# One stretch of 64x64 matmuls per unit in an attention-then-mixer kernel

## The chip, the cores and the metric

The kernel runs on one core of one Trainium2 chip. The metric is the time of one execution on the device in microseconds (us). The core has a matrix engine (PE, TensorE, whose weight loads are profiled apart as PEld), a vector engine (DVE), a scalar engine (ACT), POOL (GpSimd), which here starts the loads, and SP (SyncE), which here starts transposing DMAs and stores. PE writes into PSUM, which DVE and ACT read.

## The reference

Eight batches of 448 tokens, 12 heads of 64 and thus 768 columns:

```
attn = sigmoid(q k^T / 8 - log 448)            # q, k, v: (8, 12, 448, 64), no softmax
x    = attn v, heads side by side              # (8, 448, 768)
h    = relu(x^T w_tok1) w_tok2                 # tokens: 448 -> 256 -> 448
u    = x + h^T
out  = u + relu(u w_ch1) w_ch2                 # channels: 768 -> 1536 -> 768
```

## The kernel before

Tokens lie as 7 blocks (j) of 64. A batch is done in three units (u = 0, 1, 2) of four heads each: head pair hi (0, 1) of two groups g (0, 1). So there are 24 units, numbered c = 3b + u. Operands are fp16, sums fp32.

The first stage of a unit: **qk** (L153) multiplies, for each j, a 64-token block of k with all of q: four matmuls with 64 rows and 64 columns of weights, each in its own quarter of the array (called a quad below), and 448 columns streamed. Each fills one of two PSUM tiles "qk"; ACT reads it through the sigmoid (L168) into att. **av** (L178) sums att times v over the 7 blocks, a quad for each; DVE casts the two sums into xT (L197) and copies the last 64 tokens once more behind them (L201). **xtrans_dma** (L211) transposes xT by a DMA on SP into xn. **tok1** (L233) multiplies by w_tok1: from unit 4 on its 64-token remainder is one quad (L254, with_scores) and the rest full 128x128 matmuls (L265); ACT applies ReLU (L279). **ytrans** (L281) multiplies by w_tok2 with full matmuls (L286), and DVE adds x (L293), which gives u, two of six 128-column slices per unit.

The second stage of a batch, once all of u is there: **ch1** (L311), 12 products cb of six full matmuls with 448 columns (L318), DVE ReLU to h2 (L326); **ch2** (L333), six products (t, half) of 12 full matmuls with 384 columns (L341), DVE adds u (L351) from un, the transposed u that **utrans** (L298) makes by a DMA on SP; and **ch2_last** (L374), the last 64 tokens, in pairs of 128x64 matmuls (L386, adds L411). Stores go out on SP.

The order is written out by hand (manual schedule): each engine works in the order of the code. The loop of L609 does for each c: scores 0 and 1, av of unit c-1, score 2, a share of second-stage pieces (work(1)), scores 3 and 4, the remainder quad and tok1 of unit c-2, work(2), scores 5 and 6, work(3), ytrans of unit c-2. So each unit enters the 64x64 arrangement three times. `stage2` deals the second stage of a batch in pieces of three matmuls, about a third of its weight for each unit (`shares`), from u=2 of the next batch on.

Behind a piece, a step of `through_dma` may be dealt: DVE copies k and q of the next batch into another order (relayout, L106, three for each), and then a DMA on SP transposes them (L119). When q's is there, POOL copies two of its elements (gate, L680), and behind that starts the loads of v for the next batch and k and q for the one after it.

PSUM has eight banks: four for the two qk tiles, four under the tag "m" with bufs=4 that everything else takes in turn.

Of the kernel before, what the change touches and what calls it, by code (L numbers as in the profile page):

```python
# [26 lines left out]
def kernel(  # L27
# [45 lines left out]

    raw, rel, tr = {}, {}, {}
# [60 lines left out]
    def pe_transpose(b, t, u, j0=0, j1=NJ, on_scalar=False):  # L135
        if j0 == 0:
            tps[t] = pp.tile([128, NJ, 128], FP16, tag="m", bufs=4, name=f"tp_{t}_{b}_{u}")
        ps = tps[t]
        for j in range(j0, j1):
            for hi in range(2):  # L140
                nc.tensor.transpose(  # L141
                    out=ps[64 * hi : 64 * hi + 64, j, :],
                    in_=raw[b, t][:, u, hi, j, :],
                    identity=ident[:, :],
                )
        dst, src = tr_tile(b, t)[:, u, j0:j1, :], ps[:, j0:j1, :]
        if on_scalar:
            nc.scalar.activation(out=dst, in_=src, func=COPYF)
        else:
            nc.vector.tensor_copy(out=dst, in_=src)  # L150
# [27 lines left out]
    def av(b, u, j0=0, j1=NJ):  # L178
        if j0 == 0:
            xa[b, u] = [  # L180
                pp.tile([128, 512], FP32, tag="m", bufs=4, name=f"xa_{b}_{u}_{g}")
                for g in range(2)
            ]
        ps = xa[b, u]
        for j in range(j0, j1):
            for g in range(2):
                for hi in range(2):
                    nc.tensor.matmul(  # L188
                        out=ps[g][64 * hi : 64 * hi + 64, 0:S],
                        lhsT=raw[b, "v"][64 * g : 64 * g + 64, u, hi, j, :],  # L190
                        rhs=att[b, u][64 * g : 64 * g + 64, hi, j, :],
                        start=(j == 0),
                        stop=(j == NJ - 1),
                    )
        if j1 == NJ:
            for g in range(2):
                nc.vector.tensor_copy(  # L197
                    out=xTs[b % 2][:, u, g, 0:S], in_=ps[g][:, 0:S]
                )
            if NU * b + u >= N_FIRST:  # L200
                nc.vector.tensor_copy(  # L201
                    out=xTs[b % 2][:, u, :, S:512], in_=xTs[b % 2][:, u, :, S - 64 : S]
                )
# [13 lines left out]
    def xtrans(b, u):  # L217
        ps = pp.tile([128, 4, 2, 128], FP16, tag="m", bufs=4, name=f"xb_{b}_{u}")
        for g in range(2):
            for t in range(4):  # L220
                nc.tensor.transpose(  # L221
                    out=ps[:, t, g, :],
                    in_=xTs[b % 2][:, u, g, 128 * t : 128 * t + 128],
                    identity=ident[:, :],
                )
        nc.vector.tensor_copy(
            out=xn_tile(b)[:, u, :, :, :].rearrange("s g t d -> s t g d"),
            in_=ps[:, :, :, :],
        )
# [3 lines left out]
    def tok1(b, u, relu_on_vector=False, tcbs=range(2), with_scores=False):  # L233

        if tcbs[0] == 0:
            if u == 0:
                h1[b] = pa.tile(
                    [128, 2, 2, NU, 128], FP16, tag="h1", bufs=2, name=f"h1_{b}"
                )
            if with_scores:  # L240
                tks[b] = [
                    pp.tile([128, 2, 2, 128], FP32, tag="m", bufs=4, name=f"tk_{b}_{u}_{tcb}")[
                        :, 0, :, :
                    ]
                    for tcb in range(2)
                ]
            else:
                one = pp.tile([128, 2, 2, 128], FP32, tag="m", bufs=4, name=f"tk_{b}_{u}")
                tks[b] = [one[:, tcb, :, :] for tcb in range(2)]
        ps = tks[b]  # L250
        for tcb in tcbs if with_scores else []:
            part = slice(64 * tcb, 64 * tcb + 64)
            for g in range(2):
                nc.tensor.matmul(  # L254
                    out=ps[tcb][64 * g : 64 * g + 64],
                    lhsT=w1[part, 3, 128 * tcb + 64 * g : 128 * tcb + 64 * g + 64],
                    rhs=xn[b][part, u, :, 3, :],
                    start=True,
                    stop=False,
                )  # L260
        for tcb in tcbs:
# [10 lines left out]
        for tcb in tcbs:  # L272
            dst, src = h1[b][:, tcb, :, u, :], ps[tcb]
            if relu_on_vector:
                nc.vector.tensor_scalar(
                    out=dst, in0=src, scalar1=0.0, scalar2=None, op0=MAX
                )
            else:
                nc.scalar.activation(out=dst, in_=src, func=RELU)  # L279

    def ytrans(b, u):  # L281
        for g in range(2):
            db = NU * g + u
            ps = pp.tile([128, 512], FP32, tag="m", bufs=4, name=f"yt_{b}_{db}")
# [26 lines left out]
    def ch1(b, cb, d0=0, d1=NDB):  # L311
        if cb == 0 and d0 == 0:
            h2[b] = pa.tile([128, NCB, S], FP16, tag="h2", bufs=1, name=f"h2_{b}")
        if d0 == 0:
            acc[b, cb] = pp.tile([128, 512], FP32, tag="m", bufs=4, name=f"c1_{b}_{cb}")
# [9 lines left out]
        if d1 == NDB:  # L325
            nc.vector.tensor_scalar(  # L326
                out=h2[b][:, cb, :], in0=ps[:, 0:S], scalar1=0.0, scalar2=None, op0=MAX
            )

# [3 lines left out]
    def ch2(b, t, half, n0=0, n1=NCB):  # L333
        cols = slice(DH * half, DH * half + DH)
        if n0 == 0:
            if half == 0:
                outs[b, t] = pa.tile([128, D], FP32, tag="outs", bufs=4, name=f"o_{b}_{t}")
            acc[b] = pp.tile([128, 512], FP32, tag="m", bufs=4, name=f"c2_{b}_{t}_{half}")
# [9 lines left out]
        if n1 < NCB:  # L348
            return
        if b in un:  # L350
# [6 lines left out]
        else:  # L357
            for n in range(NU):
                nc.tensor.matmul(  # L359
                    out=ps[:, 128 * n : 128 * n + 128],  # L360
                    lhsT=uts[b % 2][:, NU * half + n, 128 * t : 128 * t + 128],
                    rhs=ident[:, :],
                    start=False,
                    stop=(n == NU - 1),
                )
# [7 lines left out]

    def ch2_last(b, n0=0, n1=NCB):  # L374
        final = b == B - 1
        if n0 == 0:
            acc[b] = [
                pp.tile([128, 512], FP32, tag="m", bufs=4, name=f"c2_{b}_3_{g}")
# [107 lines left out]
    def stage2(b):  # L486
        for cb in range(NCB):
            for d in range(0, NDB, 3):
                yield 3 * S, lambda cb=cb, d=d: ch1(b, cb, d, d + 3)
        groups = [(t, half) for t in range(3) for half in range(2)]  # L490
        if b == 0:
            groups.sort(key=lambda g: g[1])
        for t, half in groups:
            for n in range(0, NCB, 3):
                yield 3 * DH, lambda t=t, half=half, n=n: ch2(b, t, half, n, n + 3)
        for n in range(0, NCB, 3):
            yield 3 * DH, lambda n=n: ch2_last(b, n, n + 3)

# [12 lines left out]
    def new_heat():  # L511
        heat[0] = pp.tile([128, 512], FP32, tag="m", bufs=4, name="heat")
# [91 lines left out]

    ON_DMA = range(N_FIRST, N_CYCLES)
    ON_PE = 2 * NU + 1
    starts = [N_FIRST] + [NU * b + 5 for b in range(1, B - 1)] + [N_CYCLES + 1]
    pending, copies = [], []
    for c in range(N_FIRST, N_CYCLES + 1):  # L609
        b, u = divmod(c, NU)  # L610
        here = c < N_CYCLES
        before = divmod(c - 1, NU)
        mixed = [n for n in (c - 2, c - 1) if (n == c - 1) != (n in ON_DMA) or not here]
        if c in starts:
            lot = starts.index(c)
            first = c
            pending = list(stage2(lot))[4 if c == N_FIRST else 0 :]
            total = sum(w for w, f in pending)


            shares = {0: [9, 9, 6, 6], 1: [12, 9, 9]}.get(lot, [10, 10, 10])
            spent = [0, 0]

        def work(share):
            goal = 3 * sum(shares[: c - first]) + share * shares[c - first]
            while pending and spent[0] < total * goal / 90:
                w, f = pending.pop(0)
                f()
                spent[0] += w
                spent[1] += 1  # L630
                if copies and (c < 3 * NU or spent[1] % 2 == 0):
                    copies.pop(0)()

        if here:
            qk(b, u, 0)
            qk(b, u, 1)
# [3 lines left out]
        if here:  # L640
            qk(b, u, 2)
        if c == 2 * NU + 2:
            copies += through_dma(3, 0)[NU + 1 :]
        work(1)
# [5 lines left out]
        if here:  # L650
            qk(b, u, 3)
            qk(b, u, 4)
        early = [n for n in mixed if here and n < c - 1]
        for n in early:
            tok1(*divmod(n, NU), with_scores=True)
# [4 lines left out]
        work(2)  # L660
        if u == 2 and b > 1:
# [4 lines left out]
        if here:  # L666
            qk(b, u, 5)
            qk(b, u, 6)
        if b > 2 and u == 0 and b + 1 < B:
            copies = through_dma(b + 1, 0)  # L670
        work(3)
        if c == N_FIRST:
            nc.gpsimd.dma_start(out=w1[64:128, 3, :], in_=tok_rows[NJ - 1])
        for n in mixed:
# [4 lines left out]
        if here and u == 2 and b + 1 < B:  # L679
            nc.gpsimd.tensor_copy(  # L680
                out=gate[:, :], in_=tr[b + 1, "q"][:, NU - 1, NJ - 1, 126:128]
            )
            if b > 1:
                load(b + 1, "v", v, 0, NU)
            for t, src in (("k", k), ("q", q)):
                if b + 2 < B:
                    load(b + 2, t, src, 0, NU)
    assert not copies
    utrans(B - 1)
    for w, f in pending:  # L690
# [33 lines left out]
```

## Time and profile before

| | before |
|---|---|
| three runs, us | 368.52, 368.86, 370.37 (median 368.86) |
| profiled execution: time / span, us | 368.45 / 366.7 |
| PE busy, matmuls | 359.0 us (98%), 3308 |
| PEld (weight loads) busy | 194.5 us (53%), 3308 |
| DVE busy, instructions | 186.0 us (51%), 343 |
| ACT busy, instructions | 172.5 us (47%), 214 |
| granted PE clock in the 40 slices | 9 tenths or more throughout |
| L318 (ch1) / L341 (ch2) / L161 (qk) / L188 (av) busy, us | 115.3 / 100.3 / 53.1 / 37.4 |
| read from and written to device memory | 43.45 MB / 11.01 MB |

The span runs from the first to the last instruction of the profiled execution. A row of a timeline gives start, duration, engine, line, what is written and read, and the count of like instructions merged; in brackets the idle time of the engine before it and what ended that. A row of waits gives who waited for whom, the total in us, the number of times and the longest. A row of the chain gives start, duration and what the end of the kernel depended on then. PE's instructions overlap: the end of each is modelled, so the distance of starts tells the pace.

### The profile page before, as it was taken

The numbers are of one execution on the slowest core, as the hardware profiler recorded it, in microseconds if no ns is written. First come the engines' busy times: TensorE is split into PE (matmuls) and PEld (weight loads), VectorE is DVE, ScalarE is ACT, GpSimd is POOL, SyncE is SP. The second block draws the span as 40 slices with busy tenths as digits, with TensorE's granted clock in tenths as the row PEclk, the third lists the DMA queues.
The fourth block names the chain that finished last, engine by engine and source line by source line (L and its number), as shares of the span: only waits on it lengthen the run. The fifth ranks groups of instructions, "written<-read, shape, count | busy, mean of one in ns | idle before, by whom it ended". The sixth has DMA issues, their size and how long they took to land.

```text
span 366.7 us, 7619 instructions
## 1 busy us (share of the span) xinstructions
PE 359.0 (98%) x3308; PEld 194.5 (53%) x3308; DVE 186.0 (51%) x343; ACT 172.5 (47%) x214; POOL 52.6 (14%) x91
## 2 busy tenths in 40 slices
PE   8899999999999999999999999999999999999995
PEld 5555555555555554555455554555445555555563
DVE  3366647258455456465455455473463355444531
ACT  2995565665455455455455445445545544000000
POOL 8865500110310040002100040000100000000000
PEclk9999999999999999999999999999999999999999
DMA  8999999999995999779991999749931344136014
GB/s 145 170 190 206 203 204 188 133 195 212 192 188 110 197 170 193 98 146 194 181 183 45 176 186 192 104 96 203 196 60 33 84 93 88 30 84 154 0 43 109
DMA packets 103953, 52.01 MB, mean 142 GB/s; under 512 B 76016, under 2 KB 100848, under 8 KB 103920
## 3 DMA queue, kind: packets, MB, share of 16 engines
q1 hardware_dynamic: 78880, 29.70, 43.3%
q0 software_dynamic: 24816, 21.50, 38.1%
q8 instruction: 26, 0.43, 0.5%
q10 hardware_dynamic: 224, 0.33, 0.3%
q14 instruction: 7, 0.06, 0.1%
HBM read 43.45 MB, written 11.01 MB: 149 GB/s over the span
## 4 chain that ended last, share of the span: by engine, by line
PE 94%; ACT 4%; DVE 1%; issue 0%
PE c L318 30%; PE c L341 26%; PE qk L161 10%; PE xa L188 8%; PE tk L265 5%; PE yt L286 5%; PE c L386 5%; ACT att L168 3%; PE heat L503 1%; PE tp_k L141 1%; PE tk L254 1%; PE tp_q L141 1%; PE xb L221 0%; DVE xT L197 0%; PE c L359 0%
## 5 line engine op out<-in xcount | busy, mean ns | idle before, releaser
L168 ACT ACTIVATE att<-qk,att_bias 128x896 f16<-128x896 f32 x168 | 158.4, 1008 | 130.8 <-PE qk L161 130.8
L318 PE MATMUL c<-ut,c 128*128 128x448 f16 x576 | 115.3, 353 | 0.0
L341 PE MATMUL c<-c,h 128*128 128x384 f16 x576 | 100.3, 326 | 0.0
L326 DVE TENSOR_SCALAR h<-c 128x448 f16<-128x448 f32 x96 | 59.7, 624 | 59.6 <-PE c L318 58.7
L318 PEld LDWEIGHTS <-c 128*128 128x128 f16 x576 | 54.2, 98 | 55.2 <-issue 9.1
L341 PEld LDWEIGHTS <-h 128*128 128x128 f16 x576 | 54.5, 98 | 40.6 <-issue 6.8
L161 PE MATMUL qk<-tr_q,tr_k 64*64 64x448 f16 x672 | 53.1, 361 | 2.1 <-ACT att L168 2.0
L351 DVE TENSOR_TENSOR o<-un,c 128x384 f32<-128x384 f16 x42 | 23.3, 554 | 58.7 <-PE c L341 58.6
L188 PE MATMUL xa<-att,raw_v 64*64 64x448 f16 x672 | 37.4, 350 | 0.0
L197 DVE CAST xT<-xa 128x448 f16<-128x448 f32 x48 | 27.7, 619 | 17.7 <-PE xa L188 17.7
L161 PEld LDWEIGHTS <-tr_k 64*64 64x64 f16 x672 | 15.8, 104 | 28.3 <-issue 25.6
L293 DVE TENSOR_TENSOR ut<-xT,yt 128x448 f16<-128x448 f16 x48 | 27.4, 614 | 5.9 <-PE yt L286 5.7
L188 PEld LDWEIGHTS <-raw_v 64*64 64x64 f16 x672 | 22.5, 107 | 9.9 <-issue 1.1
L680 POOL COPY gate<-tr_q 128x2 f16<-128x2 f16 x6 | 1.1, 183 | 182.9 <-DMA tr_q<-rel_q 163.0
L286 PE MATMUL yt<-w,h 128*128 128x448 f16 x96 | 22.1, 353 | 0.0
L265 PE MATMUL tk<-xn,w 128*128 128x256 f16 (+1 forms) x156 | 21.7, 274 | 0.0
L279 ACT ACTIVATE h<-tk 128x256 f16<-128x256 f32 x42 | 13.8, 387 | 13.4 <-PE tk L265 13.4
L407 ACT ACTIVATE o<-c 64x384 f32<-64x384 f32 x1 | 0.5, 485 | 40.6 <-PE c L397 40.6
L265 PEld LDWEIGHTS <-w 128*128 128x128 f16 (+1 forms) x156 | 13.3, 97 | 8.3 <-issue 6.2
L386 PE MATMUL c<-c,h 128*64 128x384 f16 x192 | 17.3, 328 | 0.0
L95 POOL DMA_DIRECT2D raw_q<-in_q_dram x26 | 16.7, 658 | 2.3 <-POOLq L708 0.8
L95 POOL DMA_DIRECT2D raw_k<-in_k_dram x24 | 15.3, 657 | 7.4 <-DMA c<-in_moe_w_ch_dram 4.3
(49 smaller groups left out, 136.0 us busy)
## 6 DMA issues: line engine op xcount, KB each, us to landing
out_dram<-o SPq DMA_DIRECT2D x48, 192.0 KB, 2.8
c<-in_moe_w_ch_dram POOLq DMA_DIRECT2D x4, 1152.0 KB, 15.3
raw_v<-in_v_dram POOLq DMA_DIRECT2D x12, 336.0 KB, 6.8
raw_k<-in_k_dram POOLq DMA_DIRECT2D x10, 336.0 KB, 9.3
raw_q<-in_q_dram POOLq DMA_DIRECT2D x10, 336.0 KB, 12.3
raw_q<-in_q_dram POOLq DMA_DIRECT2D x14, 112.0 KB, 6.2
out_dram<-o SPq DMA_DIRECT2D x15, 96.0 KB, 2.9
raw_k<-in_k_dram POOLq DMA_DIRECT2D x12, 112.0 KB, 6.1
```

The lines of the kernel that those rows point to most:

```text
L95: nc.gpsimd.dma_start(out=dst.rearrange("p u hi j e -> p (u hi) (j e)"), in_=heads.rearrange("h (p j) e -> p h (j e)", j=NJ),)
L161: nc.tensor.matmul(out=ps[64 * g : 64 * g + 64, hi, 0:S], lhsT=tr[b, "k"][64 * hi : 64 * hi + 64, u, j, 64 * g : 64 * g + 64], rhs=tr[b, " ...
L168: nc.scalar.activation(out=att[b, u][:, :, j, :], in_=ps[:, :, 0:S], func=SIGMOID, bias=bias_t[:, :], scale=att_scale,)
L188: nc.tensor.matmul(out=ps[g][64 * hi : 64 * hi + 64, 0:S], lhsT=raw[b, "v"][64 * g : 64 * g + 64, u, hi, j, :], rhs=att[b, u][64 * g : 64 ...
L197: nc.vector.tensor_copy(out=xTs[b % 2][:, u, g, 0:S], in_=ps[g][:, 0:S])
L265: nc.tensor.matmul(out=ps[tcb], lhsT=w1[rows, t, cols], rhs=xn[b][rows, u, :, t, :], start=(t == 0 and not with_scores), stop=(t == (2 if ...
L286: nc.tensor.matmul(out=ps[:, 0:S], lhsT=h1[b][:, tcb, g, u, :], rhs=w2[:, tcb, :, :], start=(tcb == 0), stop=(tcb == 1),)
L293: nc.vector.tensor_tensor(out=uts[b % 2][:, db, 0:S], in0=xTs[b % 2][:, u, g, 0:S], in1=ps[:, 0:S], op=ADD)
L318: nc.tensor.matmul(out=ps[:, 0:S], lhsT=c1[:, BY_UNIT[d], 128 * cb : 128 * cb + 128], rhs=uts[b % 2][:, BY_UNIT[d], 0:S], start=(d == 0), ...
L326: nc.vector.tensor_scalar(out=h2[b][:, cb, :], in0=ps[:, 0:S], scalar1=0.0, scalar2=None, op0=MAX)
L341: nc.tensor.matmul(out=ps[:, 0:DH], lhsT=h2[b][:, cb, 128 * t : 128 * t + 128], rhs=c2[:, cb, cols], start=(cb == 0), stop=(cb == NCB - 1 ...
L386: nc.tensor.matmul(out=ps[g], lhsT=h2[b][:, n, 384:448], rhs=c2[:, n, DH * g : DH * g + DH], start=(n == 0), stop=(n == NCB - 1 and not ad ...
```

## The change

From unit 9 (batch 3) on, the loop is another one. Each unit has one stretch in the 64x64 arrangement: all seven scores, av of the unit before, the remainder quad of the token product, and a pair of second-stage products that are cut into quads. `quads` issues four 64x64 matmuls: in turn 0 row half r of the weights goes to product r, in turn 1 to product 1 - r; the first turn runs over all slices before the second. A pair in ch1 is done wholly so (six slices, two turns); a pair in ch2 has eight of its twelve slices in quads and four as full matmuls after the stretch (`rest`).

The second stage is dealt anew: all of ch1 in u=2, ch2 for t=0 and ch2_last in the next u=0, ch2 for t=1 and 2 in u=1. The steps of copies and transposes for k and q stand behind every second piece of u=0, 1 and 2. utrans is issued early in u=2, ahead of that unit's xtrans_dma. Unit 8 does all of ch1 of batch 1, with three visits as before.

The four "m" banks get names m0 to m3 with one buffer each, and `bank` hands them out in turn, skipping a bank with an open sum; from unit 9 on at_bank is set by hand, so that pairs and second-stage products begin at m2 and av, the token product and ytrans at m0 and m1.

```diff
+    at_bank, open_bank = [0], [None]
+    def bank(shape, dtype, name):
+        if at_bank[0] == open_bank[0]:
+            at_bank[0] = (at_bank[0] + 1) % 4
+        tag = f"m{at_bank[0]}"
+        at_bank[0] = (at_bank[0] + 1) % 4
+        return pp.tile(shape, dtype, tag=tag, bufs=1, name=name)
...
-                pp.tile([128, 512], FP32, tag="m", bufs=4, name=f"xa_{b}_{u}_{g}")
+                bank([128, 512], FP32, f"xa_{b}_{u}_{g}")
...
+    def quads(ps, n, turn, lhsT, rhs, first, last):
+        for r in range(2):
+            p = r ^ turn
+            part = slice(64 * r, 64 * r + 64)
+            for m in (0, 64):
+                nc.tensor.matmul(
+                    out=ps[p][m : m + 64, 0:n],
+                    lhsT=lhsT(p, part, m),
+                    rhs=rhs(p, part),
+                    start=(first and turn == 0),
+                    stop=(last and turn == 1),
+                )
+    def ch1_pair(b, cb):
+        if cb == 0:
+            h2[b] = pa.tile([128, NCB, S], FP16, tag="h2", bufs=1, name=f"h2_{b}")
+        ps = [bank([128, 512], FP32, f"c1_{b}_{cb + p}") for p in range(2)]
+        def step(turn, d):
+            quads(
+                ps,
+                S,
+                turn,
+                lambda p, part, m: c1[
+                    part, BY_UNIT[d], 128 * (cb + p) + m : 128 * (cb + p) + m + 64
+                ],
+                lambda p, part: uts[b % 2][part, BY_UNIT[d], 0:S],
+                d == 0,
+                d == NDB - 1,
+            )
+            if turn == 1 and d == NDB - 1:
+                for p in range(2):
+                    ch1_out(b, cb + p, ps[p])
+        turns = [[lambda t=t, d=d: step(t, d) for d in range(NDB)] for t in range(2)]
+        return turns[0], turns[1], lambda: None
...
+    def ch2_pair(b, t):
+        outs[b, t] = pa.tile([128, D], FP32, tag="outs", bufs=4, name=f"o_{b}_{t}")
+        ps = [bank([128, 512], FP32, f"c2_{b}_{t}_{p}") for p in range(2)]
+        n_quads = 8
+        def step(turn, n):
+            quads(
+                ps,
+                DH,
+                turn,
+                lambda p, part, m: h2[b][part, n, 128 * t + m : 128 * t + m + 64],
+                lambda p, part: c2[part, n, DH * p : DH * p + DH],
+                n == 0,
+                False,
+            )
+        def rest():
+            for p in range(2):
+                for n in range(n_quads, NCB):
+                    nc.tensor.matmul(
+                        out=ps[p][:, 0:DH],
+                        lhsT=h2[b][:, n, 128 * t : 128 * t + 128],
+                        rhs=c2[:, n, DH * p : DH * p + DH],
+                        start=False,
+                        stop=(n == NCB - 1),
+                    )
+                ch2_out(b, t, p, ps[p])
...
+    ONE_RUN = 3 * NU
...
-    for c in range(N_FIRST, N_CYCLES + 1):
+    for c in range(N_FIRST, ONE_RUN):
...
-            shares = {0: [9, 9, 6, 6], 1: [12, 9, 9]}.get(lot, [10, 10, 10])
...
+            if c == N_FIRST:
+                pending, shares = stage2(0, by_half=True)[4:], [9, 9, 6, 6]
+            else:
+                pending, shares = list(pieces_ch1(1)), [30]
...
+        if c + 1 == ONE_RUN:
+            at_bank[0] = 0
         for n in mixed:
             ytrans(*divmod(n, NU))
...
+    for c in range(ONE_RUN, N_CYCLES):
+        b, u = divmod(c, NU)
+        before, ahead = divmod(c - 1, NU), divmod(c - 2, NU)
+        lot = b - 1 if u == 2 else b - 2
+        at_bank[0] = 2
+        if u == 2:
+            turn0, turn1, rest = ch1_pair(lot, 0)
+            work = pieces_ch1(lot, 2)
+        elif u == 0:
+            turn0, turn1, rest = ch2_pair(lot, 0)
+            work = pieces_last(lot)
+        else:
+            turn0, turn1, rest = ch2_pair(lot, 1)
+            work = pieces_ch2(lot, [(2, 0), (2, 1)])
+        part = len(turn1) * 2 // 3
+        qk(b, u, 0)
+        qk(b, u, 1)
+        for f in turn0:
+            f()
+        qk(b, u, 2)
+        if u == 2:
+            utrans(b - 1)
+        av(*before, 0, 4)
+        qk(b, u, 3)
+        av(*before, 4, NJ)
+        xtrans_dma(*before)
+        qk(b, u, 4)
+        for f in turn1[:part]:
+            f()
+        qk(b, u, 5)
+        for f in turn1[part:]:
+            f()
+        at_bank[0] = 0
+        tok_tail(*ahead)
+        qk(b, u, 6)
+        rest()
+        tok1(*ahead, with_scores=True)
+        at_bank[0] = 2
+        if u == 0 and b + 1 < B:
+            copies = through_dma(b + 1, 0)
+        for n, (w, f) in enumerate(work):
+            f()
+            if copies and n % 2 == 1:
+                copies.pop(0)()
+        at_bank[0] = 0
+        ytrans(*ahead)
+        if u == 2 and b + 1 < B:
+            gated_loads(b)
...
+    c, lot = N_CYCLES, B - 2
+    groups = [(t, half) for t in range(3) for half in range(2)]
+    work = [f for w, f in [*pieces_ch2(lot, groups), *pieces_last(lot)]]
+    before, ahead = divmod(c - 1, NU), divmod(c - 2, NU)
+    av(*before)
+    xtrans_dma(*before)
+    for f in work[:12]:
+        f()
+    tok1(*ahead)
+    for f in work[12:16]:
+        f()
+    tok1(*before)
+    for f in work[16:20]:
+        f()
+    ytrans(*ahead)
+    ytrans(*before)
     utrans(B - 1)
```

`tok_tail` is the remainder quad taken out of tok1, `ch1_out` and `ch2_out` are the DVE outputs taken out of ch1 and ch2, and `pieces_ch1`, `pieces_ch2` and `pieces_last` are the parts of `stage2`. `gated_loads` is the gate with its loads, put into a function.

## The prediction

> **What bounds the kernel now.** I read the page's busy shares and its chain first, then the chain in order of time, the timeline of one steady stretch, and last the waits and the landings of the loads.
>
> ```profile
> PE 359.0 (98%) x3308; PEld 194.5 (53%) x3308; DVE 186.0 (51%) x343; ACT 172.5 (47%) x214; POOL 52.6 (14%) x91
> ...
> PE 94%; ACT 4%; DVE 1%; issue 0%
> ```
>
> PE carries the span; ACT and DVE are half idle. From the waits, and from the chain in order of time:
>
> ```profile
> PE qk L161 <- ACT att L168: 2.0, 5, 0.5
> ```
>
> ```profile
> 25.91 0.51 PE tp_k L141 x14
> ...
> 334.93 13.72 PE c L318 x72
> 348.66 11.70 PE c L341 x72
> ```
>
> PE waits for ACT only in the first 21 us; later it never waits. A full-array matmul of 448 columns takes 13.72/72 = 0.19 us (single starts lie 0.189 apart), one of 384 columns 11.70/72 = 0.1625. So time can go only where PE spends more than these pitches. The timeline of a steady stretch (start, duration, engine, line, count):
>
> ```profile
> 211.44 0.93 PE L286 MATMUL yt<-w,h 128*128 128x448 f16 x4
> 211.55 1.14 DVE L411 TENSOR_TENSOR o<-un,c 64x384 f32<-64x384 f16 x2 [1.52 <-PE c L386]
> ...
> 225.44 0.92 PE L286 MATMUL yt<-w,h 128*128 128x448 f16 x4
> ...
> 226.29 0.57 PE L161 MATMUL qk<-tr_q,tr_k 64*64 64x448 f16 x8
> ...
> 226.70 1.49 PE L188 MATMUL xa<-att,raw_v 64*64 64x448 f16 x28
> 226.79 2.80 ACT L168 ACTIVATE att<-qk,att_bias 128x896 f16<-128x896 f32 x3 [2.36 <-PE qk L161]
> ...
> 228.31 3.58 PE L318 MATMUL c<-ut,c 128*128 128x448 f16 x18
> ...
> 231.82 0.57 PE L161 MATMUL qk<-tr_q,tr_k 64*64 64x448 f16 x8
> ...
> 232.44 0.83 PE L265 MATMUL tk<-xn,w 128*128 128x256 f16 x6
> ```
>
> From 225.44 to 228.31 there are 4 full matmuls and 10 quads (four 64x64 matmuls side by side: 3 score quads, 7 of L188), 14 x 0.189 = 2.65 us, but 2.87 passed. By single starts, entering the 64x64 mode costs 0.093 (282 ns for 189), the first quad 0.025 (214), leaving 0.103 and the first full matmul 0.011: **0.232 us per visit**. From 228.31 to 231.82, 18 full matmuls take 3.51 for 3.40: the same 0.093 at the next entry. A unit (one c) has three visits.
>
> **The change, part by part.** The profiled execution took 368.45 us (span 366.7, 1.75 around it); the median of the runs shown, 368.86, is 0.4 above it.
>
> *Visits.* Units 9 to 23, fifteen, go from three visits to one: 30 x 0.232 = **-6.96 us**. The visits to 128x64 for L386 stay.
>
> *Quads for full matmuls.* A pair in ch1 is 12 quads of 448 columns in place of 12 full matmuls, five times; L188 shows such quads 189 ns apart with fresh weights each: 0. A ch2 pair is 16 quads of 384 columns for 16 full ones (8 stay full in rest), ten times. No quad of 384 columns is in the trace. From below, 384 columns take 162.5 (L341, and pairs of L386 in 128x64 mode); from above, L188's 189, with as many instructions for a quad. 160 x 0.0265 = 0 to +4.24 us. I take 0: eight instructions in 162.5 ns are 20 ns each, and the transposes (L141, 56 ns for two loads and two matmuls) issue one per 14 ns. PE gets 660 more matmuls and loads; the densest 5.2 us now holds 220 instructions, a run will hold some 250.
>
> The Trainium skill ("TensorE: Matmul & The Clock Gate", Part 3) says that a weight load overlaps a running matmul only if it is for another row group. By that, all 220 new quads would pay for their loads. This trace disagrees: L188 reloads the same tile every 189 ns.
>
> *Scores paced by ACT.* ACT starts 0.50 after the first score quad (226.29 to 226.79) and runs at 0.897 per tile (2.80 for three with its tail); a score quad needs the tile two before it read, 1.06 after that read began (8.65 to 9.71 early on). So scores 2 to 6 cannot start before 1.56, 2.45, 3.35, 4.25, 5.14 in the run. PE would be there, in a ch2 run, at 1.70, 2.65, 3.41, 4.41, 5.20: no wait. In a ch1 run at 1.54, 2.50, 3.26, 4.30, 4.97: waits of 0.02, 0.09, 0.17, in all 0.28. Only batch 7 pays it (**+0.28**); in the others a later start, next, covers it.
>
> *Joint from u=1 to u=2.* The copies of k and q (L106, 0.53 each in a row) are dealt behind every second piece, so one stands on DVE between the add of the unit's last product (L351) and the two adds of L293. Counted from the next unit's first score: L351 ends at -0.10 (it starts 0.36 after its last matmul, and lasts 0.55), the copy at 0.47, the L293 adds at 1.04 and 1.61. The sixth slice (d=5) of the ch1 pair reads the second add's result; PE is there at 0.403 + 5 x 0.189 = 1.35 and waits to 1.68: 0.33. All PE work behind it waits; the casts and ACT have slack. Batches 3 to 6 have copies: 4 x 0.33 = **+1.32**.
>
> *Joint from u=0 to u=1.* Now L386 to L286 to L161 with two L411 adds ending 0.39 after the first score (212.69 against 212.30). The new copy goes behind them (0.96), the adds of L293 end at 1.53 and 2.10. The run's av takes banks 0 and 1 that these adds read, at 1.89; it waits to 2.16. The pair's bank 2 waits 0.04 for L411, so 0.27 in all: 4 x 0.27 + 0.04 = **+1.12**. From u=2 to u=0 no copy is left: adds end at 1.04, no wait.
>
> *Banks.* In a run tail and tok1 want banks 0 and 1 after both casts: last av quad + 0.40 + 1.17 + 0.05, 1.62 later; PE arrives 1.70 later in a ch1 run, 1.87 in a ch2 run. At the end of unit 8 the counter is set to 0, and counting allocations from the start the last ch1 sum sits in bank 1, read until 1.02 after its last matmul starts, while the second ytrans wants it at 0.57: **+0.5** once. Elsewhere round robin as before: bounds 0 to +0.2 for a unit, from the shown L326 (0.62).
>
> *Queues.* On SP the transpose of u (L300) moves ahead of that of x (L212) in u=2, and the k and q copies and transposes move from u=0 and 1 to u=0, 1 and 2, two, four and two of eight steps. SP is held up to 13 us by L300 while loads run (217.32), else 3.7. L300 now starts when no load runs, x's transpose is behind it by at most 4 us and is read a unit later. tr_q is issued about 8.7 into u=2 and lands 5.8 later (207.67 to 213.43): 14.5 of 18.4, so the next scores don't wait. The gate on POOL and the six loads behind it move from the start of u=2 to 14.6 into it:
>
> ```profile
> 213.55 0.18 POOL L680 COPY gate<-tr_q 128x2 f16<-128x2 f16 x1 [37.78 <-DMA tr_q<-rel_q]
> ...
> 215.29 1.35 POOL L95 DMA_DIRECT2D raw_k<-in_k_dram  x2
> ...
> 217.32 13.22 SPq L300 DMA_TRANSPOSE un<-ut  x1
> ```
>
> The second half of k landed 226.05, 12.5 after the gate: 27.1, which is 8.7 into the next u=0, where DVE's copy of k waits for it at 7.4 and must be done by 9.74 (L411). Cost 0, margin 0.4 us.
>
> *Tail.* Unit 24 and the last batch have the same pieces in another order: 0.
>
> Sum: -6.96 + 0.28 + 1.32 + 1.12 + 0.5 = -3.74; 368.45 - 3.74 = 364.7. As the median was 0.4 above the profiled execution, I say **365.0 us**.
>
> **Rivals.**
> 1. *Joints free.* If DVE clears sooner or the waits overlap, all 6.96 stays: 361.5 to 363. For it: each wait is 0.3 us, less than one DVE copy, so a copy that is dealt one piece earlier would clear it. Against: in every stretch read, DVE does its work in the order of the code. 0.10.
> 2. *Quads of 384 columns run at 189.* +4.24: 369. For it: twice the weight loads of L386; against: the 14 ns of the transposes. 0.10.
> 3. *More joints wait* (ACT behind ReLU, casts late by the 0.08 margin of the ch1 run, named banks), 0.2 more in each of 15 units: +3.0, 367 to 370. 0.14.
> 4. *Slower: k lands late.* DVE in u=0 is stuck on the copy of k; L411, the adds, and then av of the next run move by as much, in units 12, 15, 18. Each us beyond the 0.4 costs 3 us; it beats the gain when k is 1.25 + 0.4 = 1.65 us later than reckoned, and shows as slower from 2.3 us: 371 and more. For it: the gates of 130.27 saw k at 143.78, 13.5 later, 1 us worse. Against: L300, which shared those loads' time, is gone from there. 0.08.
> 5. *Weight loads are not hidden* in the new quads: 220 x 0.107 (the load row of 64x64) = +23.5: 388. L188 speaks against. 0.03; this is the case that the skill's sentence above describes.
>
> **How the numbers follow.** Forecast 0.55, its own range 363 to 367. A measurement tells 0.5% (1.84 us) from no change: faster is below 367.0. Forecast, rival 1 and 0.03 of rival 3 make 0.68 faster; rival 2 and 0.09 of rival 3 make 0.19 same; rivals 4 and 5 and 0.02 of rival 3 make 0.13 slower. The range 362.4 to 369.8 leaves out rivals 4 and 5 and half of 1.
>
> **What would show it.** One entry to 64x64 per unit from unit 9; PE busy share unchanged. The quads of ch2_pair 162 ns apart. Gaps of 0.33 before the last slices of the ch1 pair's first turn, released by DVE's L293 line, and of 0.27 before av in u=1; none in u=0. k's landing before 9 us into u=0. Wrong, if quads of 384 lie over 180 apart, if DVE waits for raw_k, or if ACT releases scores by more than 0.3 in a ch2 run.

## The result, and the profile after

The changed kernel takes 366.68 us (median of 13 runs, 366.38 to 368.61) against 368.76 for the kernel before (13 runs): a ratio of 0.9949, with a 95% interval of 0.9931 to 0.9967. That is 2.1 us, where 3.7 were forecast. The profiled executions, 366.46 and 368.45, differ by 1.99, and it is this difference that is taken apart below. Some executions of most kernels here take 1.5 to 2 us longer than the rest, at a mean granted clock of 0.993 to 0.995 in place of 0.997 to 1.0; the medians are over all, and one such execution, that of the fixed turn alone, is the one profiled below (its granted clock is 0.50 to 0.65 between 20 and 24 us).

The page of the changed kernel, busy shares and the head of the chain:

```profile
span 364.7 us, 8938 instructions
...
PE 354.8 (97%) x3968; PEld 207.2 (57%) x3968; DVE 186.2 (51%) x343; ACT 171.3 (47%) x214; POOL 52.8 (14%) x91
...
PE 89%; DMA 4%; POOL 4%; ACT 1%; DVE 0%; issue 0%; POOLq 0%
```

PE still carries the span, with 660 matmuls more. Its share of the chain fell from 94% to 89%, and loads came in with 8%. Before one believes that the loads are the matter now, the waits of PE must be read (who waited for what: us in total, times, longest):

```profile
PE qk L174 <- ACT att L181: 2.0, 5, 0.5
...
PE c L333 <- DVE h L345: 0.7, 1, 0.7
...
PE tp_q L154 <- DMA raw_q<-in_q_dram: 0.7, 1, 0.7
...
PE tp_q L154 <- DVE xT L210: 0.5, 1, 0.5
...
PE yt L300 <- DVE h L345: 0.3, 1, 0.3
```

Only the first row was there before, with the same 2.0. The other four are new, and three of the four lie before 50 us, in a part of the kernel where the order of the work was not changed. (Waits of a single quarter of the array don't appear here as idle time of PE; they show only in the length of a stretch.)

The stretch of a unit u=0 in the timeline (start, duration, engine, line, count of like instructions), PE alone:

```profile
148.15 0.57 PE L174 MATMUL qk<-tr_q,tr_k 64*64 64x448 f16 x8
148.55 1.47 PE L357 MATMUL c<-c,h 64*64 64x384 f16 x32
149.85 0.36 PE L174 MATMUL qk<-tr_q,tr_k 64*64 64x448 f16 x4
150.04 0.93 PE L201 MATMUL xa<-att,raw_v 64*64 64x448 f16 x16
...
153.23 0.28 PE L260 MATMUL tk<-xn,w 64*64 64x256 f16 x4
153.34 0.36 PE L174 MATMUL qk<-tr_q,tr_k 64*64 64x448 f16 x4
153.63 1.15 PE L462 MATMUL c<-c,h 128*128 128x384 f16 x6
```

One entry, one way out, 5.48 us from 148.15 to 153.63. The eight quads of 384 columns start at 148.55 and the next score at 149.85: 1.30/8 = 0.1625 each, the pace of full matmuls of that size. 14 quads of 448 columns at 0.189, 16 at 0.1625, one of 256 at 0.109 and 0.128 for the first quad and the way out make 5.48: this stretch waits for nothing. From unit 9 on one batch takes 41.4 us (230.26 to 271.66 between the ytrans of u=2), where it took 42.2 (225.61 to 310.07 for two).

Matched matmul by matmul against the kernel before, PE is 0.66 us late at the q transpose of 24.73, 1.37 late at that of 31.82 (some of which it makes good), 2.18 late at a ch1 matmul at 48.38, and then steadily so up to unit 8. (0.09 of this is there ahead of the first of these waits.)

### The profile page after: what moved, and what is told of

Same layout as the page of the kernel before. It is cut to its first block, busy times and chain, and to the rows that moved or that the text cites. A ratio compares the mean times of both kernels' runs of the same rounds, so it can differ in the third digit from the quotient of the medians.

```text
span 364.7 us, 8938 instructions
## 1 busy us (share of the span) xinstructions
PE 354.8 (97%) x3968; PEld 207.2 (57%) x3968; DVE 186.2 (51%) x343; ACT 171.3 (47%) x214; POOL 52.8 (14%) x91
## 4 chain that ended last, share of the span: by engine, by line
PE 89%; DMA 4%; POOL 4%; ACT 1%; DVE 0%; issue 0%; POOLq 0%
PE c L333 27%; PE c L402 15%; PE c L357 11%; PE qk L174 9%; PE xa L201 8%; PE yt L300 5%; PE tk L279 5%; PE c L486 5%; PE c L462 4%; DMA raw_q<-in_q_dram 2%; DMA raw_v<-in_v_dram 2%; POOL raw_q L108 1%; POOL raw_k L108 1%; POOL raw_v L108 1%; ACT att L181 1%
## 5 line engine op out<-in xcount | busy, mean ns | idle before, releaser
L181 ACT ACTIVATE att<-qk,att_bias 128x896 f16<-128x896 f32 x168 | 155.6, 1015 | 119.7 <-PE qk L174 119.0
L333 PE MATMUL c<-ut,c 128*128 128x448 f16 x516 | 100.6, 353 | 0.7 <-DVE h L345 0.7
L333 PEld LDWEIGHTS <-c 128*128 128x128 f16 x516 | 49.6, 98 | 48.4 <-issue 4.4
L174 PE MATMUL qk<-tr_q,tr_k 64*64 64x448 f16 x672 | 60.3, 357 | 2.1 <-ACT att L181 2.0
L402 PE MATMUL c<-c,h 128*128 128x384 f16 x336 | 58.1, 326 | 0.0
L402 PEld LDWEIGHTS <-h 128*128 128x128 f16 x336 | 32.1, 98 | 21.7 <-issue 1.8
L201 PE MATMUL xa<-att,raw_v 64*64 64x448 f16 x672 | 41.0, 350 | 0.0
L174 PEld LDWEIGHTS <-tr_k 64*64 64x64 f16 x672 | 22.8, 105 | 21.4 <-issue 15.6
L357 PE MATMUL c<-c,h 64*64 64x384 f16 x640 | 32.0, 323 | 0.0
L357 PEld LDWEIGHTS <-h 64*64 64x64 f16 x640 | 19.9, 107 | 8.2 <-DVE o L511 1.5
```

The source lines that it names most:

```text
L174: nc.tensor.matmul(out=ps[64 * g : 64 * g + 64, hi, 0:S], lhsT=tr[b, "k"][64 * hi : 64 * hi + 64, u, j, 64 * g : 64 * g + 64], rhs=tr[b, " ...
L181: nc.scalar.activation(out=att[b, u][:, :, j, :], in_=ps[:, :, 0:S], func=SIGMOID, bias=bias_t[:, :], scale=att_scale,)
L201: nc.tensor.matmul(out=ps[g][64 * hi : 64 * hi + 64, 0:S], lhsT=raw[b, "v"][64 * g : 64 * g + 64, u, hi, j, :], rhs=att[b, u][64 * g : 64 ...
L333: nc.tensor.matmul(out=ps[:, 0:S], lhsT=c1[:, BY_UNIT[d], 128 * cb : 128 * cb + 128], rhs=uts[b % 2][:, BY_UNIT[d], 0:S], start=(d == 0), ...
L357: nc.tensor.matmul(out=ps[p][m : m + 64, 0:n], lhsT=lhsT(p, part, m), rhs=rhs(p, part), start=(first and turn == 0), stop=(last and turn = ...
L402: nc.tensor.matmul(out=ps[:, 0:DH], lhsT=h2[b][:, cb, 128 * t : 128 * t + 128], rhs=c2[:, cb, cols], start=(cb == 0), stop=(cb == NCB - 1 ...
```

## The experiments

### Banks by release order in the first units

The theory was that the four named banks, dealt in a fixed turn, make PE wait in the first 86 us: tp_q of unit 3, for one, gets the bank of xa, whose cast on DVE has only begun, while the bank of yt is free. With one tag and bufs=4, the next user before got a free buffer. The timeline of the changed kernel there:

```profile
24.05 1.16 DVE L210 CAST xT<-xa 128x448 f16<-128x448 f32 x2 [0.29 <-PE xa L201]
...
24.73 0.58 PE L154 MATMUL tp_q<-ident,raw_q 128*64 128x128 f16 x14 [0.53 <-DVE xT L210]
```

PE starts when the first of the two casts ends (24.05 + 0.62). At 31.82 the same pair of instructions stands, and the profile names the load of raw_q; but that half of q had landed by 22.7, and the cast there runs from 31.15 and frees the bank at about 31.77. So I took the bank for the cause there as well.

```diff
+    free, used = [0, 1, 2, 3], {}    # a bank is appended to free behind its last reader in the code
...
     def bank(shape, dtype, name):
+        if by_release[0]:        # units 0 to 8
+            used[name] = free.pop(0)
+            return pp.tile(shape, dtype, tag=f"m{used[name]}", bufs=1, name=name)
...
-        if c + 1 == ONE_RUN:
-            at_bank[0] = 0
```

> Up to unit 8 the four banks go to the next user in the order in which their last readers stand in the code, as before the change; from unit 9 on the changed kernel as it is. Theory A (the fixed turn of the banks costs the first 86 us some 2.2 us, at the two q transposes near 24 and 31 us and at the ch1 sum near 47 us, and 0.6 at the end of unit 8): 366.7 - 2.2 - 0.6 = 363.9. Rival B (these waits only take the place of others, for the loads or for ACT, in a stretch that ACT and the loads pace): within 0.5 of 366.7.

Measured: 364.73 us (6 runs; ratio to the kernel before 0.9893, 0.9867 to 0.9919), 1.95 less than the changed kernel. The whole delay of the first 86 us is gone, beyond 0.2 us that this execution is late from 6 us on. The wait that the profile had put down to the load of raw_q went with it. But the 0.5 of unit 8 did not go; it moved, grown to 0.7, to the first stretch of unit 9, as the timeline shows:

```profile
104.17 1.14 DVE L323 TENSOR_TENSOR ut<-xT,yt 128x448 f16<-128x448 f16 x2
...
104.28 0.57 PE L185 MATMUL qk<-tr_q,tr_k 64*64 64x448 f16 x8
...
105.36 0.84 PE L375 MATMUL c<-c,h 64*64 64x384 f16 x16 [0.51 <-DVE ut L323]
```

ytrans of unit 8 now sits in the banks where the first pair begins, and the pair waits for its adds: that stretch lasts 6.19 in place of 5.48. Theory A holds for the first 86 us; its sum of 363.9 was off by the joint that it only moved.

### The fixed turn alone, in the kernel before

```diff
-            acc[b, cb] = pp.tile([128, 512], FP32, tag="m", bufs=4, name=f"c1_{b}_{cb}")
+            acc[b, cb] = bank([128, 512], FP32, f"c1_{b}_{cb}")    # and so for every user of "m"
+            keep_open(b != 0 or cb > 1)
```

> The kernel before with nothing changed but the banks: four names, handed out in turn, with the bank of an open sum skipped. Theory A: the first 86 us become 2.2 us longer, and the later units, whose users come in other numbers, lose something between 0 and 2: 371 to 373. Rival B: 368.8.

Measured: 370.90 us (10 runs; ratio 1.0053, 1.0036 to 1.0071), 2.0 slower than the kernel before. The waits of PE between 20 and 60 us, with the lines of that kernel:

```profile
PE tp_q L154 <- DVE xT L210: 1.2, 2, 0.7
...
PE c L332 <- DVE h L341: 0.7, 1, 0.7
```

They are the same three waits as in the changed kernel, and this time both transposes are put down to the cast. So the naming of the banks alone costs 2.0 us, the size of theory A's first 86 us. The later units lose nothing: matched matmul by matmul, its profiled execution is 2.0 us behind the kernel before ahead of the first of these waits, 4.14 behind them and 4.12 at the end. So the time stays just under the 371 that theory A gave as its least.

### The copies a piece earlier

```diff
-            if copies and n % 2 == 1:
+            if copies and n % 2 == 0:
```

> The changed kernel with the steps of copies behind the first, third, ... piece in place of the second, fourth, ..., so that no copy stands on DVE between a unit's last product and its ytrans adds. Theory A (the stretch of u=1 is 0.34 longer with the copy than without it, 5.88 against 5.54 us, and that of u=2 is 5.46 with and without it, since ACT's pace hides it there): only u=1 gains, 4 x 0.34 = 1.4: 365.3. Rival B (the prediction as it was made: u=2 loses 0.33 to the copy as well and 0.28 to ACT only without it): 1.1 from u=1 and at most 0.2 from u=2, so 365.4, and the stretch of u=2 gets 0.05 shorter; the trace tells them apart, not the time. Rival C (the copy is not the cause): 366.7.

Measured: 365.25 us in the profiled execution, against 366.46; the median is 366.16 (6 runs, three at 365.1 to 365.3 and three at 367.1; ratio 0.9922, 0.9892 to 0.9951). The stretches tell more than the time. First the changed kernel at the start of a u=1, then this kernel at the same place:

```profile
158.62 0.57 PE L174 MATMUL qk<-tr_q,tr_k 64*64 64x448 f16 x8
159.04 0.62 DVE L119 COPY rel_k<-raw_k 128x896 f16<-128x896 f16 x1
...
159.69 1.15 DVE L307 TENSOR_TENSOR ut<-xT,yt 128x448 f16<-128x448 f16 x2
...
160.58 1.26 PE L201 MATMUL xa<-att,raw_v 64*64 64x448 f16 x16
```

```profile
158.41 0.57 PE L174 MATMUL qk<-tr_q,tr_k 64*64 64x448 f16 x8
...
158.83 1.15 DVE L307 TENSOR_TENSOR ut<-xT,yt 128x448 f16<-128x448 f16 x2
...
160.37 0.93 PE L201 MATMUL xa<-att,raw_v 64*64 64x448 f16 x16
```

With the copy, the adds end 2.22 after the first score, and the four quads of av stretch from 0.93 to 1.26 us; without it they end at 1.57, and av runs through. The stretch goes from 5.88 to 5.54 in each of the four units, 1.36 in all. That of u=2 is 5.46 in both kernels: theory A, and the prediction's separate 0.33 for u=2 was no loss of its own.

### Two idle quads in u=2

The stretch of u=2 is 5.46 us long for 5.16 us of quads, here in the changed kernel:

```profile
171.22 0.57 PE L174 MATMUL qk<-tr_q,tr_k 64*64 64x448 f16 x8
...
171.57 1.14 DVE L307 TENSOR_TENSOR ut<-xT,yt 128x448 f16<-128x448 f16 x2
171.63 1.52 PE L357 MATMUL c<-ut,c 64*64 64x448 f16 x24
...
171.72 5.49 ACT L181 ACTIVATE att<-qk,att_bias 128x896 f16<-128x896 f32 x6 [4.66 <-PE qk L174]
...
176.37 0.38 PE L174 MATMUL qk<-tr_q,tr_k 64*64 64x448 f16 x4
...
176.68 0.39 PE L279 MATMUL tk<-xn,w 128*128 128x256 f16 x2
```

The question was whether ACT's pace holds it.

```diff
-        return turns[0], turns[1], lambda: None
+        return [idle, idle, *turns[0]], turns[1], lambda: None
```

> The changed kernel with two idle quads more ahead of the first turn of the ch1 pair (their sums are thrown away), in the five units u=2: 5 x 0.38 = 1.9 us more PE work. Theory A (that stretch, 5.46 long for 5.16 of work, is paced by ACT, so the idle quads fill what PE waits anyway): each stretch 5.54, 5 x 0.08 = +0.4: 367.1. Rival B (the 0.30 is lost to something that the idle quads don't fill): +1.9: 368.6.

Measured: 367.01 us (5 runs; ratio 0.9940, 0.9919 to 0.9962), 0.33 above the changed kernel for 1.9 us more work. In the timeline:

```profile
171.51 0.57 PE L174 MATMUL qk<-tr_q,tr_k 64*64 64x448 f16 x8
171.92 0.55 PE L390 MATMUL c<-ut,c 64*64 64x448 f16 x8
...
176.75 0.37 PE L174 MATMUL qk<-tr_q,tr_k 64*64 64x448 f16 x4
177.06 0.39 PE L279 MATMUL tk<-xn,w 128*128 128x256 f16 x2
```

5.55 from 171.51 to 177.06, 0.09 more than without the idle quads (L390). Five times 0.3 us of matrix work is thus free in u=2. That it is ACT's pace that sets the length follows together with the kernel of the section before, where the adds come a copy earlier and the stretch is 5.46 all the same: the sigmoids follow each other at 0.89 us, and the last score starts (176.37) just behind the end of the fifth of them (176.32), which reads its tile.

### One more visit in u=0 and u=1

```diff
...
         tok_tail(*ahead)
+        if u != 2:
+            rest(one=True)      # one full matmul of the first product
         qk(b, u, 6)
```

> The changed kernel with one full matmul of the rest of each ch2 pair moved ahead of the last score, in u=0 and u=1: ten more entries to the 64x64 arrangement, nothing else. Theory A (an entry and the way out cost 0.23 us that nothing hides): 10 x 0.23 = +2.3: 369.0. Rival B (the gain of the change came from the new dealing of the second stage and not from the visits): +0 to 0.5: 367.

Measured: 369.12 us (10 runs; ratio 1.0002, 0.9983 to 1.0021), 2.44 above the changed kernel. Where the last score is cut off by a full matmul (L462):

```profile
153.87 0.28 PE L260 MATMUL tk<-xn,w 64*64 64x256 f16 x4
154.08 0.34 PE L462 MATMUL c<-c,h 128*128 128x384 f16 x1
154.35 0.38 PE L174 MATMUL qk<-tr_q,tr_k 64*64 64x448 f16 x4
154.67 0.50 PE L462 MATMUL c<-c,h 128*128 128x384 f16 x2
```

From 154.08 to 154.35 there is 0.27 for 0.1625 of work, from 154.35 to 154.67 0.32 for 0.189. Ten visits more undo the whole gain; 0.24 each.

### The dealing of the second stage alone, in the kernel before

```diff
+        if 0 < b < B - 1:
+            groups.insert(2, None)      # ch2_last behind t=0
...
-            shares = {0: [9, 9, 6, 6], 1: [12, 9, 9]}.get(lot, [10, 10, 10])
+            shares = [9, 9, 6, 6] if lot == 0 else [15, 45 / 7, 60 / 7]
```

> The kernel before, three visits in every unit, with the second stage dealt as in the change: ch1 in u=2, ch2 for t=0 and ch2_last in u=0, the rest in u=1. Theory A (PE is the bound and the dealing moves no work off it; the kernel before loses some 0.18 at the start of units whose DVE is behind with copies, which may go or stay): 367.8 to 369.3. Rival B (a part of the gain is the dealing's, since loads and the transposes of u no longer meet): 366 to 367.5.

Measured: 370.48 us (10 runs, 368.95 to 372.50; ratio 1.0042, 1.0018 to 1.0067). That is slower than either theory had it. In the profiled execution (370.08) PE loses 1.33 us against the kernel before between unit 8 and the last batch, for the same matmuls. 0.9 of it is a single wait:

```profile
196.55 1.02 DVE L351 TENSOR_TENSOR o<-un,c 128x384 f32<-128x384 f16 x2 [4.39 <-DMA un<-ut]
197.16 0.68 PE L386 MATMUL c<-c,h 128*64 128x384 f16 x6 [0.85 <-DVE o L351]
```

L386 waits for a bank that L351 reads, and L351 has waited for the transposed u, which was issued at 174.98, among the loads, and landed only at 196.43. In the changed kernel utrans stands earlier, and the transposed u of the same batch, issued at 172.98, landed at 179.73. Another 0.4 lies at the end, between 326 and 329 us. It is not the visits: with three visits in u=0, ch2_last is now cut in two by the last scores, as here,

```profile
154.00 0.68 PE L386 MATMUL c<-c,h 128*64 128x384 f16 x6
154.61 0.57 PE L161 MATMUL qk<-tr_q,tr_k 64*64 64x448 f16 x8
```

so that the 128x64 arrangement is entered 13 times in place of 7 after unit 8, but its parts now border on the 64x64 visits directly, and the changes from one arrangement to another are 117 in place of 116. A part of the spread of the runs stays unexplained. No gain comes from dealing the pieces anew; the other half of rival B, transposes and loads that no longer meet, was not in this kernel, as it left utrans and the loads where they were.

### The copies a piece earlier, in the kernel before

```diff
-                if copies and (c < 3 * NU or spent[1] % 2 == 0):
+                if copies and (c < 3 * NU or spent[1] % 2 == 1):
```

> The kernel before with the copies behind the first, third, ... piece in place of the second, fourth, ... from unit 9 on. In the kernel before some first visits last 2.20 or 2.07 us in place of 2.02, in all 0.84 from unit 9 on, which the prediction had at nothing. Theory A (the 0.18 of the units in which copies stand on DVE ahead of the ytrans adds, four times, are the copies' doing, the 0.055 of the units behind ch2_last, five times, are not): the visits of 2.20 fall to 2.02: 368.8 - 0.7 = 368.1. Rival B (the extra comes from elsewhere, or the copies only move to another joint): 368.8.

Measured: 368.22 us (12 runs; ratio 0.9986, 0.9975 to 0.9996) against 368.79 beside it. First visits of 2.20 us fell to 2.04; there were three of them, not four as I had written. The kernel before, and then this one, in the same unit:

```profile
156.34 1.68 PE L188 MATMUL xa<-att,raw_v 64*64 64x448 f16 x28
```

```profile
156.92 1.51 PE L188 MATMUL xa<-att,raw_v 64*64 64x448 f16 x28
```

So the kernel before waited for DVE too, in the length of its av, without an idle row on PE.

### Both mended

Release order up to unit 7, then the fixed turn over the banks in the order in which they are free, so that unit 8's ytrans and unit 9's first pair both find free banks; and the copies a piece earlier.

```diff
+        if c + 1 == ONE_RUN:
+            by_release[0], at_bank[0] = False, 0
+            names[:] = free            # tag=f"m{names[at_bank[0]]}" from here on
...
-            if copies and n % 2 == 1:
+            if copies and n % 2 == 0:
```

> The changed kernel with banks by release order up to unit 7, then in a turn whose start is chosen so that ytrans of unit 8 and the first stretch of unit 9 find free banks, and with the copies a piece earlier. Theory A (three separate losses: 2.0 from the banks in the first 86 us, 0.6 to 0.7 at the joint of units 8 and 9, which the release order alone only moved from ytrans to the first pair, and 1.4 from the copies in u=1): 366.7 - 2.0 - 0.7 - 1.4 = 362.6. Rival B (the losses overlap): 363.5 to 364.5.

Measured: 362.89 us (5 runs, 362.57 to 364.79), a ratio to the kernel before of 0.9840 (0.9814 to 0.9865): 3.8 us better than the changed kernel, 6.0 better than the kernel before, and the fastest here. The losses add up nearly in full (3.8 of 4.1); no new wait came in their place. Its waits of PE:

```profile
PE qk L185 <- ACT att L192: 2.0, 5, 0.5
...
PE heat L630 <- DVE att_bias L551: 1.1, 1, 1.1
...
PE tp_k L163 <- DVE raw_k L642: 0.3, 1, 0.3
```

They are those of the start alone.

## Why the prediction was right, and where it was not

The direction, the mechanism and the range held: 365.0 was forecast, 366.68 came. The terms of the sum, with what the trace shows for each (profiled executions; stretches measured from the first score to the first full matmul behind it):

| step | predicted, us | measured, us |
|---|---|---|
| 30 visits fewer | -6.96 | -6.96 taken over; ten visits more cost 2.44, 0.24 each |
| waits at first visits of the kernel before, gone | 0 | -0.84 |
| u=2: second ytrans add, and ACT's pace | +1.60 | +1.51 (5 x 0.302) |
| u=1: copies ahead of the ytrans adds | +1.12 | +1.64 (4 x 0.395 + 0.06) |
| unit 8: second ytrans | +0.5 | +0.5 |
| first 86 us: banks (0.09 of it at the start) | 0 | +2.17 |
| sum | -3.74 | -1.98 |

The profiled executions differ by -1.99, so what the other rows leave for the visits is 6.97.

**The step that failed** is the sentence "Elsewhere round robin as before". It took the one tag with four buffers for a fixed turn. The two kernels with one part alone show otherwise: the fixed turn put into the kernel before makes it 2.0 us slower, and release order put into the changed kernel takes 1.95 off. The bounds of 0 to 0.2 for a unit were too narrow as well, since they took the ReLU of L326 for the reader that is waited for; in the first units it is the cast behind an av that ends just before the transpose, 0.5 to 0.7 each. Rival 3 named the banks too, but in the fifteen units of the new loop; there no bank made PE wait beyond the joints of the table.

**Quads of 384 columns** run at 0.1625, the lower end, chosen by the transposes' rate of instructions: rival 2 (369) is out. Every quad of L357 reloads the tiles of the quad before, each load 0.107 long, and the quads still start 0.1625 apart, so rival 5 (388) is out. The rule of the Trainium skill ("TensorE: Matmul & The Clock Gate", Part 3) that a weight load overlaps only with a matmul of another row group does not hold here.

**The joint at u=1** was the right wait at too small a size: 0.335 for the copy where 0.23 was reckoned. The adds ended 2.22 after the first score, not at 2.10. What was left out is that the wait stands within a quad: two matmuls of the first quad of av start at 160.58, the two others, which write the second bank, at 160.90. From there on the four starts of a quad lie in two pairs, 0.16 to 0.19 apart, up to the end of the stretch, where the way out must wait for the later pair.

**The joint at u=2** was counted with 0.33 in four units and ACT's pace with 0.28 in the one without copies. In fact the adds end at 1.49, PE waits 0.20 for them, and ACT's pace takes another 0.10; without the copy ACT takes 0.30 alone. The sum of the two was right to 0.1 us, but the copy costs nothing there, as the kernel with the copies a piece earlier and the one with the idle quads show.

**What was left out** on the other side: PE was said never to wait after 21 us, since no row of the waits said so. The first visits of the kernel before were 0.84 us longer than their quads in all. Without this the changed kernel would have come 0.84 less ahead, at some 367.5; that much of the nearness is luck.

**k's landing** (rival 4) was no matter: DVE never waited for raw_k, whose second half landed 0.9 to 1.2 us before its first copy (154.68 against 155.61 in unit 12). Rival 1 (the joints free) is not what happened. With mended joints the kernel comes to 362.9, inside the 361.5 to 363 that it gave, but by another sum: u=2 still pays 1.5 us to ACT's pace, and the 0.84 came on top.

## What to carry to other kernels

When buffers are renamed, cost the handing out as an edit of its own, in every part of the kernel that uses them, the untouched parts first: here a fixed turn gave a transpose the bank whose reader had just begun, while another bank was free. When PE runs in quarters, read the length of a stretch against its quads and not the rows of waits, since a wait of some quarters leaves PE "busy". And where an engine's queue is in the order of the code, put a copy that nobody waits for behind, or well ahead of, the last operation that releases the next stage.

## What the runs showed of the hardware

The quarters of the array drift apart within a stretch of quads, and then run on independently. In u=1 two matmuls of a quad waited 0.32 us for a bank (160.58 to 160.90). The next quad's first matmul came right behind (160.904, 0.14 later than at its pace), and from there the starts of each quad lay in two pairs, 0.156 to 0.186 us apart for some 20 quads, each pair at the full pace of 0.189 and 0.1625. Where one product follows another, a matmul can then start ahead of one that stands before it in the code: two of a score (L174, 163.25) started before the last of the pair's quad (L357, 163.28). In the stretch of u=2 and in u=0 the four starts of a quad lie within 0.04 us.

128x64 costs a visit what 64x64 costs: in the kernel before, a stretch of 64x64 or of 128x64 matmuls is 0.128 us longer than its matmuls at their pace, and a stretch of full ones between two such is 0.105 to 0.11 longer.
